# Moving the load, sums and splits of the first w1 chunk, and giving one product of the first feed-forward step its own PSUM bank

## The chip, the cores and the metric

The kernel runs on one core of a Trainium2 chip. TensorE (PE) multiplies into eight PSUM banks of 128 partitions by 512 float32, with its weight loads shown apart as PEld. VectorE (DVE), ScalarE (ACT) and GpSimd (POOL) do the elementwise work. SyncE (SP) issues nearly all DMAs, in program order on one queue. The metric is device time in microseconds (us) of one execution; lower is better. Each engine runs its own instructions in order, so an instruction that waits holds up everything behind it on its engine.

## The reference

The input x is 2048 tokens by 576. The output mixes a linear-attention block and an MLP with a gate of each token:

```python
x = A_x                                             # (1, 2048, 576)
g = sigmoid((x * gate_w).sum(-1, keepdims=True))
q, k, v = split(x @ wqkv)                           # 32 heads of 18
phi = lambda t: where(t > 0, t + 1, exp(t)) + 1e-6
kv = einsum("bhsd,bhse->bhde", phi(k), v);  z = phi(k).sum over tokens
a  = (einsum(phi(q), kv) / (phi(q) . z + 1e-6)) @ wo
y  = layernorm(x)
h  = gelu(y @ w1 + b1)                              # 576 -> 4608, tanh form
b  = h @ w2 + b2                                    # 4608 -> 576
out = g * a + (1 - g) * b
```

All inputs are float32. The kernel keeps that precision by splitting a factor into a high part and a remainder and adding the products high x high, high x low and low x high.

## The kernel before, in words

**Stages.** Up to about 186 us of the profiled span the kernel takes the tokens in 16 blocks of 128, projects keys and queries, and accumulates the sums of phi(k) with x. The next stage, called the wp stage here, turns these sums into one matrix wp (products with `wv`, then `project_values` with `wot`), and then runs 16 steps, `attend(0)` to `attend(15)`, which end at 279.6 us. The rest is the feed-forward: 36 steps k = 0 to 35, two passes over 18 chunks of 256 columns of w1, each pass for 1024 tokens.

**One attend step.** For step i the program issues, in this order: the five PE transposes of block i + 1 (`transpose_q`) with the ACT copies and the two DVE subtractions that make the tile `qt` out of them; the 28 matmuls of `attend(i)`, `ps<-wp,qt`; on DVE `normalize(i + 3)`, which is a reduction, a small addition and a reciprocal on `den` and one wide instruction on the accumulator; on POOL `weigh(i + 4)`, which fills `qz`; on ACT `attend_out(i)`, with a store `late_acc` on SP; and then whatever stands in the list `extra[i]`. A `qt` tile holds high parts, a tail and low parts; the low parts and the lower half of the tail come from the two DVE subtractions, and the matmuls need the tail from the ninth on.

**The first chunks of w1.** Each feed-forward step forms seven products instead of eight from 2 x 2 blocks (Strassen-Winograd), so each chunk of w1 is stored as seven blocks: four are loaded (two DMAs each, eight in all, `accs<-in_um` and `accs<-in_ue`), and four are sums or differences made on POOL by `sum_w1`, each 128x384, the last of which takes the place of a loaded block. Then ACT copies the high parts and DVE subtracts for the low parts (`split_w1`), into `wa` for four blocks and `wb` for three. The raw chunks 0 and 1 use the same place, `spare`, the free front of the tile `accs`. That place holds `xk`, an input of the `wv` products, before. Chunks 0 and 1 are loaded and summed, and chunk 0 is split and stored, inside the attend steps through the lists `extra`: load of chunk 0 at step 1, its sums at 5, its splits at 7 and 9, load of chunk 1 at 9, its sums at 11.

**y.** The normalised and split tokens of the first pass, `y`, are read back from DRAM by seven DMAs of 1280 KB (`load_y`), issued on SP before the attend steps. The place of `y` holds the projection weights of q and k until then, so most of these loads wait for the last projection.

**The feed-forward's order.** `make_up`, `make_units`, `make_w1` and others list operations with what they need and give. A planner then sets the order on every engine by estimated costs and due times: the up-products in the order of the list, the down-products (`ps<-region,h`) merged among them, ACT, DVE and POOL work by due time. A change in one operation's needs can therefore reorder the work of many later steps. In `make_up` a step takes three of the four banks 0 to 3 in turn, called X, Yb and Z: step 0 has banks 0, 1, 2 and step 1 banks 3, 0, 1.

**Step 0 of the feed-forward.** `UP_ORDER` gives the products 1, 5, 6, 2, 7, 4, 3. Product 1 goes to X, 5 to Z, 6 is added to X, 2 goes to Yb, 7 is added to X, 4 is added to X, 3 is added to Z. ACT copies X out to SBUF after product 1 (key u1), after 6 (u2) and after 7 (u3); DVE adds Yb to the first copy (q1) and Z to the third (q3). Product 4 may touch X only when u3 is done, and product 3 may touch Z only when q3 is done. After product 3 DVE adds Z to the second copy (q2). Each of the four results gets a gelu on ACT for the high part, one for the whole, and a DVE subtraction for the low part (`h<-u,h`).

Of the kernel before, what the change touches and what calls it, by code (L numbers as in the profile page):

```python
# [11 lines left out]
AF = mybir.ActivationFunctionType  # L12
# [66 lines left out]
C_OF = {1: (1, 0), 2: (1, 0), 6: (1, 1), 5: (0, 1), 7: (0, 1), 3: (1, 1), 4: (0, 0)}  # L79
W2_PLACES = [FACTORS[n][1] for n in DOWN_ORDER]  # L80
W2_GROUPS = ((0, 1), (2, 3), (4, 5), (6,))

def raw(ap):
# [27 lines left out]
def tile_gated_mix(ctx: ExitStack, tc: tile.TileContext, x, xm, xe, wm, we, wvm, wve, wo, um, ue, w2, b1, b2, gw, out):  # L113
# [22 lines left out]
    def four_times(ap, half):  # L136

        (ld, r), (st, n) = ap.ap
        return bass.AP(tensor=ap.tensor, offset=ap.offset + half * 32 * ld, ap=[[0, 4], [ld, 32], [st, n]])
# [544 lines left out]
            dve.tensor_tensor(out=kvs[:, n, at_:at_ + hi - lo], in0=kv[j][:, own], in1=mask[:, own], op=OP.mult)  # L684
    w_pairs = cycle((6, 4))

    def project_values(t):

        pw = two_of(w_pairs)
        own = [(n, j) for n, (to, j) in enumerate(PIECES) if to == t]  # L690
        for half in range(2):
            for n, j in own:
                pe.matmul(pw[:, half, :HALF], kvs[:, n], wot[:, j, half_cols(half)], start=(n == own[0][0]),
                          stop=(n == own[-1][0]))
        p = pw[:, :, :HALF]
        act.activation(halves(wp[:, t]), p, AF.Copy)
        dve.tensor_tensor(out=halves(wp[:, 5 + t]), in0=p, in1=halves(raw(wp[:, t])), op=OP.subtract)
# [47 lines left out]

    b2b = pks
    hs, wholes = {}, {}

    def wr(k):
        at_ = fresh[:, :21 * P] if k > 1 else spare[:, :21 * P]  # L750
        return at_.rearrange("p (m s n) -> p m s n", m=7, s=3)

    def load_w1(k):
        r = wr(k)
        main = um[k].rearrange("p (h t f n) -> p h t f n", h=2, t=2, f=CF)
        for f, a in ((0, A11), (1, A21)):
            for h in range(2):
                sp.dma_start(r[:, a + h, 0:2], main[:, h, :, f])
                sp.dma_start(r[:, a + h, 2], four_times(ue[k][:, f * P:(f + 1) * P], h))

    def sum_w1(k, which=range(4)):
        r = wr(k)
        for to, x0, x1, op in [((S1, A21, A22, OP.add), (S2, S1, A11, OP.subtract), (S4, A12, S2, OP.subtract),
                                (S3, A11, A21, OP.subtract))[n] for n in which]:
            pool.tensor_tensor(out=r[:, to], in0=r[:, x0], in1=r[:, x1], op=op)
# [51 lines left out]
    def split_all_w1(k, first):  # L817
        a0, a1 = FIRST_W if first else LAST_W
        for part in range(3):
            split_w1(k, a0, a1 + 1, part)  # L820

    extra = {i: [] for i in range(NT)}
    extra[1] += [lambda: load_w1(0)]
    for i, part in ((1, gates_in), (2, gates_act), (3, gates_out)):
        extra[i] += [lambda part=part: part(len(MOMENTS) - 1)]
    extra[5] += [lambda: sum_w1(0), lambda: act.activation(tiny, ones[:, 0:1], AF.Gelu_apprx_tanh)]
    extra[7] += [lambda: split_all_w1(0, True), lambda: store_w1(0, True)]
    extra[9] += [lambda: split_all_w1(0, False), lambda: load_w1(1), lambda: store_w1(0, False)]
    extra[11] += [lambda: sum_w1(1)]
    extra[13] += [lambda: sp.dma_start(b2b, everywhere(b2, D))]  # L830

    for i in range(NT):
# [45 lines left out]
    def op(engine, f, cols=0, needs=(), gives=(), port=False, take=None, give=(), ns=None, tail=None, more=0, by=None,  # L878
           early=0):
        if ns is None:  # L880
            a, b, c = COST[engine]
            ns = a + b * cols + more
            tail = ns + c
        o = Op(engine, f, ns, tail, needs, gives, port, take, give, by)
        o.early = early
        ops.append(o)
        for key in o.gives:
            assert key not in makers, key
            makers[key] = o
        if take:  # L890
            lines[take[0]].append(o)
        return o
# [26 lines left out]
    def add_to(to, x, y):  # L919
        dve.tensor_tensor(out=to, in0=x, in1=y, op=OP.add)  # L920
# [27 lines left out]
    def make_up(k):  # L948
# [3 lines left out]
        w1_in = lambda n: w1_key(k, FACTORS[n][0])  # L952
        seven = k in SEVEN
        base = lambda n: y_in(n) + w1_in(n)
        for n in UP_ORDER:
            if n == 1:
                up_product(k, 1, X, True, base(1) + free(X))
                if k:
# [27 lines left out]
                up_product(k, 4, X, False, base(4) + [("u3", k)])  # L986
                gelu_op(k, H21, lambda: ps[:, X], [("p", k, 4)], not seven, False)
            if n == 3:
                up_product(k, 3, Z, False, base(3) + [("q3", k)])
                op(DVE, lambda: add_to(us((k, H12)), ps[:, Z], us((k, H12))), SB, needs=[("p", k, 3), ("u2", k)],  # L990
                   gives=[("q2", k)])
                gelu_op(k, H12, lambda: us((k, H12)), [("q2", k)], True, True)
            if seven and n in (4, 3):
# [520 lines left out]
```

## Time and profile before

| | us |
|---|---|
| median of 3 runs | 1127.2 |
| lowest and highest | 1127.04 and 1127.81 |
| time of the profiled execution | 1125.78 |
| its span | 1124.1 |
| PE busy in the span | 1108.0 |
| DVE busy | 888.7 |
| ACT busy | 642.6 |
| POOL busy | 385.9 |

The page lists busy time by engine, then groups of instructions. In a timeline a row gives the start, the busy time, the engine and the operation with its count, and in brackets the idle time before it on that engine with the engine and tile that ended it. SPq rows are the DMA issues on SP's queue. Nearly all instructions are recorded through one helper, so they carry line 109; they are told apart by their tiles. `ps` is PSUM, `accs` the tile whose front is `spare`, `region` the split w2, `fresh` the raw chunks of w1 and w2 from the feed-forward on.

### The profile page before, as it was taken

Reading aid. Unit: us, or ns where it says so; the run is one execution under the profiler, and the core shown is the slowest. Engines: PE = TensorE matmul, PEld = TensorE weight load, DVE = VectorE, ACT = ScalarE, POOL = GpSimd, SP = SyncE. Lnnn points to the kernel's source line nnn. Section 1 sums busy time; section 2 is a strip of 40 time slices with the busy share of each in tenths; the row PEclk is TensorE's granted clock in tenths of the full one; section 3 lists DMA queues with packets and bytes.
Section 4 is the critical chain, followed back from the end, with each engine's and each line's share of the span. In section 5 each row is a group of like instructions: output and inputs, shape, how many; then the busy total and the mean of one; then the engine's idle time right before and its main releaser. Section 6 shows DMA issues by size and latency. Waiting matters only on the chain.

```text
span 1124.1 us, 18584 instructions
## 1 busy us (share of the span) xinstructions
PE 1108.0 (99%) x6766; PEld 1003.5 (89%) x6766; DVE 888.7 (79%) x1369; ACT 642.6 (57%) x1153; POOL 385.9 (34%) x325
## 2 busy tenths in 40 slices
PE   9999999999999999999999999999999999999998
PEld 8999889999889888898988888888888888888888
DVE  4567685896787889979979997877887778778888
ACT  6667565453556665666756666345554555455542
POOL 2111112342334252634515453315433443344430
PEclk9999999999999999999999999999999999999999
DMA  6269853554636546473564549764445444444432
GB/s 177 64 88 286 168 171 141 225 204 160 210 122 213 187 162 213 150 267 126 186 221 154 197 166 373 280 234 129 120 123 147 127 115 127 138 127 124 120 109 85
DMA packets 109086, 189.42 MB, mean 169 GB/s; under 512 B 8892, under 2 KB 69068, under 8 KB 104898
## 3 DMA queue, kind: packets, MB, share of 16 engines
q1 hardware_dynamic: 108114, 187.49, 52.7%
q8 instruction: 53, 0.87, 0.3%
q10 hardware_dynamic: 720, 0.74, 0.2%
q14 instruction: 39, 0.32, 0.1%
q0 software_dynamic: 160, 0.01, 0.1%
HBM read 121.40 MB, written 66.80 MB: 167 GB/s over the span
## 4 chain that ended last, share of the span: by engine, by line
PE 72%; DVE 14%; ACT 4%; DMA 4%; issue 3%; POOL 2%; SPq 1%; ACTq 0%; DVEq 0%; POOLq 0%
PE ps L109 72%; DVE accs L109 3%; DVE h L109 3%; DMA fresh<-in_w 2%; DVE region L109 2%; SPq L109 1%; DVE wa L109 1%; POOL u L109 1%; DVE wb L109 1%; DVE den L109 1%; ACT h L109 1%; ACT u L109 1%; POOL fresh L109 1%; DVE u L109 1%; DMA w1d<-wb 0%
## 5 line engine op out<-in xcount | busy, mean ns | idle before, releaser
L109 PEld LDWEIGHTS ps<-region,h 128*128 128x128 f32 x3144 | 453.7, 188 | 45.9 <-DVE accs L109 10.0
L109 PE MATMUL ps<-region,h 128*128 128x288 f32 x3144 | 480.9, 296 | 4.0 <-DVE accs L109 2.0
L109 DVE TENSOR_TENSOR accs<-ps,accs 128x576 f32<-128x576 f32 x336 | 250.3, 752 | 89.8 <-PE ps L109 87.0
L109 POOL TENSOR_TENSOR fresh<-fresh 128x288 f32<-128x288 f32 (+1 forms) x164 | 173.8, 1066 | 406.2 <-DMA fresh<-in_w 332.0
L109 PE MATMUL ps<-y,wa 128*128 128x512 f32 x1008 | 269.7, 393 | 1.4 <-ACT ps L109 1.1
L109 PE MATMUL ps<-y,wb 128*128 128x512 f32 x756 | 204.3, 396 | 1.2 <-ACT u L109 1.0
L109 PEld LDWEIGHTS ps<-y,wa 128*128 128x128 f32 x1008 | 176.3, 188 | 27.2 <-DVE wa L109 1.7
L109 DVE TENSOR_TENSOR h<-u,h 128x512 fp32r<-128x512 f32 x222 | 177.1, 811 | 7.2 <-ACT u L109 4.3
L109 POOL TENSOR_TENSOR u<-u 128x512 f32<-128x512 f32 x104 | 152.3, 1465 | 88.1 <-DVE h L109 46.8
L109 PEld LDWEIGHTS ps<-y,wb 128*128 128x128 f32 x756 | 132.5, 188 | 24.7 <-ACT u L109 1.6
L109 PE MATMUL ps<-y 128*128 128x288 f32 (+1 forms) x896 | 126.9, 297 | 3.6 <-DVE acc L109 2.2
L109 ACT ACTIVATE u<-ps 128x512 f32<-128x512 f32 x73 | 43.7, 598 | 151.4 <-PE ps L109 151.4
L109 PEld LDWEIGHTS ps<-y 128*128 128x128 f32 x896 | 122.3, 188 | 7.0 <-DVE acc L109 3.4
L109 DVE TENSOR_TENSOR region<-fresh,region 128x576 fp32r<-128x576 f32 x120 | 107.8, 898 | 2.4 <-ACT region L109 1.9
L109 ACT ACTIVATE region<-fresh 128x576 fp32r<-128x576 f32 x120 | 73.9, 628 | 33.9 <-PE ps L109 33.9
L109 ACT ACTIVATE h<-ps,b1s 128x512 fp32r<-128x512 f32 x45 | 30.9, 687 | 81.9 <-PE ps L109 81.8
L109 ACT ACTIVATE h<-u,b1s 128x512 fp32r<-128x512 f32 x73 | 52.6, 721 | 32.7 <-DVE u L109 32.7
L109 ACT ACTIVATE h<-u 128x512 fp32r<-128x512 f32 x104 | 60.2, 622 | 12.4 <-POOL u L109 12.2
L109 PE MATMUL ps<-wp,qt 128*128 128x288 f32 x448 | 63.6, 298 | 1.2 <-DVE qt L109 1.2
L109 DVE TENSOR_TENSOR u<-ps,u 128x512 f32<-128x512 f32 x73 | 50.2, 688 | 15.7 <-ACT u L109 12.1
L109 DVE TENSOR_TENSOR wa<-fresh,wa 128x512 fp32r<-128x512 f32 x64 | 50.6, 791 | 14.8 <-ACT wa L109 13.9
L109 PEld LDWEIGHTS ps<-wp,qt 128*128 128x128 f32 x448 | 60.0, 188 | 1.7 <-DVE qt L109 1.7
(122 smaller groups left out, 994.9 us busy)
## 6 DMA issues: line engine op xcount, KB each, us to landing
w1d<-wa SPq DMA_DIRECT2D x17, 1280.0 KB
wa<-w1d SPq DMA_DIRECT2D x68, 320.0 KB
fresh<-in_w SPq DMA_DIRECT2D x70, 288.0 KB
y<-yd SPq DMA_DIRECT2D x14, 1280.0 KB
w1d<-wb SPq DMA_DIRECT2D x17, 960.0 KB
wb<-w1d SPq DMA_DIRECT2D x51, 320.0 KB
yd<-ystage SPq DMA_DIRECT2D x28, 320.0 KB
fresh<-in_um SPq DMA_DIRECT2D x64, 128.0 KB
```

Of the source, the lines that this page charges most:

```text
L109: return lambda *args, **kwargs: self.tc.keep_in_program_order(op(*args, **kwargs))
```

## The change

Four things change.

1. `load_w1(0)`, the eight DMAs of the first raw chunk, is issued right after the masked copies of the `wv` products, ahead of `project_values` and ahead of the seven loads of `y`. Before, it came in `extra[1]`, behind the loads of `y` and two stores.
2. The four sums of chunk 0 stand in `extra[0]` to `extra[3]`, one in each, instead of all four in `extra[5]`.
3. The splits of chunk 0 move from the steps 7 and 9 to 10 and 12; with the second goes the load of chunk 1 (9 to 12), and its sums move from 11 to 14.
4. In feed-forward step 0, product 3 comes before product 4 and opens bank 3 instead of being added to Z. It waits for no copy. DVE adds bank 3 to the second copy (new key q4) and then Z (q2), one DVE addition more. Step 1, whose X is bank 3, waits for q4 before its first product.

```diff
+W1_AT = (10, 12, 14)
+FIRST_ORDER = (1, 5, 6, 2, 7, 3, 4)
...
     w_pairs = cycle((6, 4))
+    def wr(k): ...
+    def load_w1(k): ...
+    load_w1(0)
+
     def project_values(t):
...
-    extra[1] += [lambda: load_w1(0)]
     for i, part in ((1, gates_in), (2, gates_act), (3, gates_out)):
         extra[i] += [lambda part=part: part(len(MOMENTS) - 1)]
-    extra[5] += [lambda: sum_w1(0), lambda: act.activation(tiny, ones[:, 0:1], AF.Gelu_apprx_tanh)]
-    extra[7] += [lambda: split_all_w1(0, True), lambda: store_w1(0, True)]
-    extra[9] += [lambda: split_all_w1(0, False), lambda: load_w1(1), lambda: store_w1(0, False)]
-    extra[11] += [lambda: sum_w1(1)]
+    for n in range(4):
+        extra[n] += [lambda n=n: sum_w1(0, (n,))]
+    extra[5] += [lambda: act.activation(tiny, ones[:, 0:1], AF.Gelu_apprx_tanh)]
+    extra[W1_AT[0]] += [lambda: split_all_w1(0, True), lambda: store_w1(0, True)]
+    extra[W1_AT[1]] += [lambda: split_all_w1(0, False), lambda: load_w1(1), lambda: store_w1(0, False)]
+    extra[W1_AT[2]] += [lambda: sum_w1(1)]
...
-        for n in UP_ORDER:
+        for n in UP_ORDER if k else FIRST_ORDER:
...
-                up_product(k, 3, Z, False, base(3) + [("q3", k)])
-                op(DVE, lambda: add_to(us((k, H12)), ps[:, Z], us((k, H12))), SB, needs=[("p", k, 3), ("u2", k)],
+                up_product(k, 3, Z if k else 3, not k, base(3) + ([("q3", k)] if k else bank_users[3]))
+                if not k:
+                    op(DVE, lambda: add_to(us((k, H12)), ps[:, 3], us((k, H12))), SB, needs=[("p", k, 3), ("u2", k)],
+                       gives=[("q4", k)])
+                    bank_users[3] = [("q4", k)]
+                op(DVE, lambda: add_to(us((k, H12)), ps[:, Z], us((k, H12))), SB, needs=[("p", k, 3), ("u2", k)] if k else [("p", k, 5), ("q4", k)],
                    gives=[("q2", k)])
```

Three places in the order of the built programs follow. On POOL in the attend steps (`qz` is `weigh`, `accs<-accs` a sum of a w1 chunk) the order before is

```order
L109 TENSOR_TENSOR qz<-accs,pks 128x576 x8
L109 TENSOR_TENSOR qz<-acc_93,pks 128x576
L109 TENSOR_TENSOR qz<-acc_94,pks 128x576
L109 TENSOR_TENSOR accs<-accs 128x384 x4
L109 TENSOR_TENSOR qz<-acc_95,pks 128x576
```

and after

```order
L110 TENSOR_TENSOR qz<-accs,pks 128x576 x5
L110 TENSOR_TENSOR accs<-accs 128x384
L110 TENSOR_TENSOR qz<-accs,pks 128x576
L110 TENSOR_TENSOR accs<-accs 128x384
L110 TENSOR_TENSOR qz<-accs,pks 128x576
L110 TENSOR_TENSOR accs<-accs 128x384
L110 TENSOR_TENSOR qz<-accs,pks 128x576
L110 TENSOR_TENSOR accs<-accs 128x384
L110 TENSOR_TENSOR qz<-acc_93,pks 128x576
```

The block of four sums is gone from between the tenth and eleventh `weigh`; each sum now stands between two of them, earlier.

On DVE around the first split of chunk 0 (`den` and `acc` are `normalize`, `qt` the subtractions that the next attend step needs) the order before is

```order
L109 SCALAR_TENSOR_TENSOR acc_95<-acc_95,den 128x576
L109 TENSOR_TENSOR wa<-accs,wa 128x4x256
L109 TENSOR_TENSOR wa<-accs,wa 64x4x128
L109 TENSOR_TENSOR qt<-ps,qt 128x512
L109 TENSOR_TENSOR qt<-ps,qt 64x128
```

and after

```order
L110 SCALAR_TENSOR_TENSOR acc_98<-acc_98,den 128x576
L110 TENSOR_TENSOR wa<-accs,wa 128x4x256
L110 TENSOR_TENSOR wa<-accs,wa 64x4x128
L110 TENSOR_TENSOR qt<-ps,qt 128x512
L110 TENSOR_TENSOR qt<-ps,qt 64x128
```

The two instructions are the same; they now stand behind the normalisation of block 13 instead of block 10. The split into `wb` moves in the same way, from behind block 12 (`acc_97`) to behind block 15 (`acc_100`).

On DVE in feed-forward step 0 (`wa` is the split of chunk 1, `u<-ps,u` the additions q3, q4 and q2, `region` the split of w2, `h` the low parts of the gelus) the order before is

```order
L109 TENSOR_TENSOR u<-ps,u 128x512
L109 TENSOR_TENSOR wa<-accs,wa 64x2x128
L109 TENSOR_TENSOR region<-fresh,region 128x2x288
L109 TENSOR_TENSOR u<-ps,u 128x512
L109 TENSOR_TENSOR h<-u,h 128x512 x3
L109 TENSOR_TENSOR region<-fresh,region 128x2x288
L109 TENSOR_TENSOR h<-u,h 128x512
```

and after

```order
L110 TENSOR_TENSOR u<-ps,u 128x512 x2
L110 TENSOR_TENSOR wa<-accs,wa 64x2x128
L110 TENSOR_TENSOR u<-ps,u 128x512
L110 TENSOR_TENSOR region<-fresh,region 128x2x288
L110 TENSOR_TENSOR h<-u,h 128x512 x2
L110 TENSOR_TENSOR region<-fresh,region 128x2x288
L110 TENSOR_TENSOR h<-u,h 128x512 x2
```

The added addition stands in front, and the first split of w2 moves behind the last addition. On PE behind step 0's products, the first down-product before is

```order
L109 MATMUL ps<-y,wb 128x512 x21
L109 MATMUL ps<-y,wa 128x512 x11
L109 MATMUL ps<-region,h 128x288 x12
L109 MATMUL ps<-y,wa 128x512 x7
L109 MATMUL ps<-region,h 128x288 x12
```

and after

```order
L110 MATMUL ps<-y,wb 128x512 x21
L110 MATMUL ps<-y,wa 128x512 x14
L110 MATMUL ps<-region,h 128x288 x12
L110 MATMUL ps<-y,wa 128x512 x4
L110 MATMUL ps<-region,h 128x288 x12
```

Three more matmuls of step 1 stand ahead of the first down-product. From step 2 on the planner's order on ACT, DVE and POOL differs in many places, by one or two positions each; on PE it differs in a few.

More of the change, by code (lines that the diff above doesn't have):

```diff
@@ L685, in tile_gated_mix, with wr, load_w1 @@
     w_pairs = cycle((6, 4))
+    def wr(k):
+        at_ = fresh[:, :21 * P] if k > 1 else spare[:, :21 * P]
+        return at_.rearrange("p (m s n) -> p m s n", m=7, s=3)
+    def load_w1(k):
+        r = wr(k)
+        main = um[k].rearrange("p (h t f n) -> p h t f n", h=2, t=2, f=CF)
+        for f, a in ((0, A11), (1, A21)):
+            for h in range(2):
+                sp.dma_start(r[:, a + h, 0:2], main[:, h, :, f])
+                sp.dma_start(r[:, a + h, 2], four_times(ue[k][:, f * P:(f + 1) * P], h))
+    load_w1(0)
     def project_values(t):
@@ L747, in tile_gated_mix @@
     hs, wholes = {}, {}
[L749 to L759, printed above, removed]
     def sum_w1(k, which=range(4)):
```

## The prediction

> **What bounds the kernel now.** I read the page's busy times first, then busy time by stretch, then PE's waits, then the timelines around the few gaps.
>
> ```profile
> PE 1108.0 (99%) x6766; PEld 1003.5 (89%) x6766; DVE 888.7 (79%) x1369; ACT 642.6 (57%) x1153; POOL 385.9 (34%) x325
> ```
>
> PE is busy for 1108.0 of 1124.1 us. The change removes no matmul, so it can only win idle time of PE, 16.1 us in all. Busy time by stretch (stretch, its length, then busy us of PE, PEld, DVE, ACT, POOL, clock, DMA share, GB/s) shows where that idle time lies:
>
> ```profile
> 188.00:206.00 18.00, 17.85 (x113) 15.32 (x111) 9.79 (x26) 5.03 (x11) 6.70 (x5) 1.00 0.00 1
> 206.00:236.00 30.00, 29.90 (x232) 29.90 (x232) 26.28 (x55) 14.36 (x35) 7.50 (x6) 1.00 0.85 324
> 236.00:279.00 43.00, 41.75 (x319) 41.06 (x318) 34.04 (x54) 19.36 (x41) 17.77 (x14) 1.00 0.44 159
> 310.00:725.20 415.20, 409.80 (x2419) 364.00 (x2417) 358.94 (x511) 260.67 (x429) 173.11 (x136) 1.00 0.58 202
> ```
>
> In the attend steps PE idles 0.10 + 1.25 us. In the long stretch from 310 to 725.2 us it idles 5.4 us, with DVE busy for 358.94/415.2 = 86%. The gaps in the part that the change touches are these rows of PE's timeline (with the row ahead of each gap):
>
> ```profile
> 248.80 1.30 PE L109 MATMUL ps<-wp,qt 128*128 128x288 f32 x8
> 250.95 1.33 PE L109 MATMUL ps<-wp,qt 128*128 128x288 f32 x8 [0.85 <-DVE qt L109]
> 258.64 1.30 PE L109 MATMUL ps<-wp,qt 128*128 128x288 f32 x8
> 260.34 1.86 PE L109 MATMUL ps<-wp,qt 128*128 128x288 f32 x12 [0.39 <-DVE qt L109]
> 285.97 1.75 PE L109 MATMUL ps<-y,wb 128*128 128x512 f32 x7
> 288.71 3.49 PE L109 MATMUL ps<-y,wb 128*128 128x512 f32 x14 [1.00 <-ACT u L109]
> 294.54 1.64 PE L109 MATMUL ps<-region,h 128*128 128x288 f32 x11
> ```
>
> In attend steps 9 and 11 the ninth matmul waits for `qt`, 0.85 and 0.39 us. In feed-forward step 0 product 4 waits 1.00 us for the copy u3.
>
> **Why the attend steps wait.** DVE's timeline in those steps, and POOL's:
>
> ```profile
> 227.67 0.19 DVE L109 TENSOR_TENSOR den<-den,den 128x32 f32<-128x32 f32 x1
> 240.35 1.01 DVE L109 TENSOR_TENSOR den<-den,den 128x32 f32<-128x32 f32 x1
> 247.91 1.93 DVE L109 TENSOR_TENSOR wa<-accs,wa 128x1024 fp32r<-128x1024 f32 x2
> 249.88 1.02 DVE L109 TENSOR_TENSOR qt<-ps,qt 128x512 fp32r<-128x512 f32 x2
> 253.84 1.02 DVE L109 TENSOR_TENSOR qt<-ps,qt 128x512 fp32r<-128x512 f32 x2
> 257.70 1.53 DVE L109 TENSOR_TENSOR wb<-accs,wb 128x768 fp32r<-128x768 f32 x2
> 259.27 1.02 DVE L109 TENSOR_TENSOR qt<-ps,qt 128x512 fp32r<-128x512 f32 x2
> ```
> ```profile
> 204.90 1.42 POOL L109 TENSOR_TENSOR qz<-accs,pks 128x576 f32<-128x576 f32 x1 [3.02 <-DVE den L109]
> 236.75 4.57 POOL L109 TENSOR_TENSOR accs<-accs 128x384 f32<-128x384 f32 x4 [7.59 <-DMA accs<-in_ue]
> 264.53 4.57 POOL L109 TENSOR_TENSOR accs<-accs 128x384 f32<-128x384 f32 x4 [7.36 <-DMA accs<-in_ue]
> ```
>
> Both waits have a split (1.93 and 1.53 us) directly ahead of the late `qt`. POOL, moreover, stood still 7.59 us for the raw chunk, with `weigh` queued behind; when the sums ran, the small `den` addition took 1.01 us instead of 0.19.
>
> **The change, part by part.** The sum is made on the profiled execution: span 1124.1, time 1125.78; the median of the runs, 1127.2, lies 1.42 above it, and the difference found is put on that median.
>
> Load of chunk 0 ahead of `y`. Eight issues are moved; SP's queue and PE's place beside it:
>
> ```profile
> 180.59 31.40 SPq L109 DMA_DIRECT2D y<-yd  x7
> 232.91 0.55 SPq L109 DMA_DIRECT2D accs<-in_ue  x1
> ```
> ```profile
> 190.64 5.66 PE L109 MATMUL ps<-accs,wv 128*126 128x126 f32 x50
> 227.42 3.95 PE L109 MATMUL ps<-wp,qt 128*128 128x288 f32 x28
> 231.67 3.96 PE L109 MATMUL ps<-wp,qt 128*128 128x288 f32 x28
> ```
>
> The load must wait for the `wv` products to leave `spare`, at 190.64 + 5.66 = 196.3. DMA moved next to nothing from 188 to 206 (share 0.00), so eight issues of about 0.55 us end near 200.7. The last load before was issued at 232.91 and released POOL at 236.75, 3.8 us later, with the `y` traffic in the way; that bounds the landing at about 204.5. The first sum stands behind a `weigh` that ends at 204.90 + 1.42 = 206.3, so POOL does not wait: cost 0. Of the seven `y` loads the first slips from 181 to about 201; the others wait for projections anyway. They have until 279 us: cost 0, with tens of us as cover. The stores `late_acc` and the moments come earlier on SP; nobody waits for them here.
>
> Sums in steps 0 to 3. Four POOL instructions of 4.57/4 = 1.14 us each. POOL is busy 7.50 of 30 us there, so POOL itself has room. On DVE each can hold up an instruction; at most 1.01 - 0.19 = 0.82 us each by the `den` row, at least 0 when they fall beside `qt` or the reduction. I take 0 on the path: a sum follows directly on a `weigh`, when DVE comes to the `qt` of the next block (1.02 us, the same with sums running or not). The Trainium skill, "SBUF — State Buffer", "Who interferes with whom", says that a DVE instruction with two SBUF inputs contends with a GpSimd instruction that reads SBUF; the 0.19 and 1.01 agree, and `qt` with its PSUM input keeps 1.02.
>
> Splits at 10 and 12. ACT's part:
>
> ```profile
> 244.34 0.74 ACT L109 ACTIVATE accs<-ps,g 128x576 f32<-128x576 f32 x1 [0.62 <-PE ps L109]
> 244.98 1.48 ACT L109 ACTIVATE wa<-accs 128x1536 fp32r<-128x1536 f32 x1
> 285.07 1.57 ACT L109 ACTIVATE wa<-accs 128x768 fp32r<-128x768 f32 x2
> ```
>
> At step 7 ACT ended the high part at 246.46, but DVE came to the low part only at 247.91, 1.45 us late, because it was behind. If DVE is on time, the split of step 10 runs like this, counted from the first matmul of the step that needs the `qt` behind it (248.80 in the old place): ACT done at -2.34, DVE split done at -0.4, `qt` done at +0.7, needed after eight matmuls at +1.30. Margin 0.6 us. Is DVE on time? Without a split its step is 253.84 - 249.88 = 3.96 us, PE's is 231.67 - 227.42 = 4.25, so it gains 0.3 us per step, and from step 12 on it has no normalisation at all. I take both waits as gone: -0.85 - 0.39 = -1.24. Bounds: 0 if the waits only move, -1.24 if all goes. The second split is 0.4 us shorter and has 1.0 us of margin.
>
> Chunk 1, three steps later. Its sums slip by about 3 x 4.25 = 12.8 us, from 264.53 to at most 277.3, done by 281.9; ACT first wants them at 285.07. Cost 0, margin 3 us; if it is gone, step 1's split is late by what is missing.
>
> Product 3 in bank 3. Product 7 ends at 285.97 + 1.75 = 287.72. Product 3 no longer waits and covers u3; both products end 0.99 us earlier. ACT shows why product 4 waited:
>
> ```profile
> 287.46 0.72 ACT L109 ACTIVATE h<-u,b1s 128x512 fp32r<-128x512 f32 x1 [0.81 <-DVE u L109]
> 288.08 0.58 ACT L109 ACTIVATE u<-ps 128x512 f32<-128x512 f32 x1
> ```
>
> The copy stood behind a gelu; it ends at 288.66, and product 4 now comes at 289.47. The added DVE addition is 0.69 us of work like its neighbours; product 1 of step 1 waits for it, but it can run from 289.5 to 290.2 and that product comes at 291.2: cost 0, at most 0.7. Late next is the first down-product. Three more matmuls of step 1 (3.49/14 = 0.25 us each) come ahead of it, so it could start at 294.54 - 0.99 + 0.75 = 294.30. It wants two low parts from DVE, the second by its sixth matmul, about 0.7 us later:
>
> ```profile
> 292.85 3.64 DVE L109 TENSOR_TENSOR h<-u,h 128x512 fp32r<-128x512 f32 x3
> ```
> ```profile
> 290.98 4.97 POOL L109 TENSOR_TENSOR fresh<-fresh 128x384 f32<-128x384 f32 x4 [21.88 <-DMA fresh<-in_ue]
> ```
>
> The low parts take 1.21 us each while POOL's sums run, so the second ends at 292.85 + 2.43 = 295.28. If POOL's sums, released by a DMA, keep that pace, the sixth matmul waits 295.28 - 295.00 = 0.28 us. If the split of w2, now ahead of the low parts, costs a turn of 1.2 us as well, the whole 0.99 is lost. I take 0.3, by the first case: -0.7. Bounds -0.99 and 0.
>
> The planner's new order. From step 2 on hundreds of rows change place on DVE and ACT without any work added. What PE waits for from 310 to 730 us (engine and tile waited for, us, times, longest):
>
> ```profile
> PE ps L109 <- ACT ps L109: 2.5, 4, 1.1
> PE ps L109 <- DVE accs L109: 2.0, 5, 0.7
> PE ps L109 <- DVE wa L109: 0.4, 1, 0.4
> PE ps L109 <- DVE wb L109: 0.2, 1, 0.2
> ```
>
> Eleven waits, 5.1 us, 0.46 on average. Nothing in the rows says whether the new order has more or fewer. I take 0, with 1.6 us to either side (three or four waits more or fewer); bounds -5.1, and above an equal +5.1 as an estimate.
>
> Sum: -1.24 - 0.7 + 0 = -1.94 us. 1127.2 - 1.9 = 1125.3; in a profiled execution a span of about 1122.2.
>
> **The rivals.**
>
> Sums against DVE. DVE is tight at step 5, behind the gate work:
>
> ```profile
> 225.83 1.02 DVE L109 TENSOR_TENSOR qt<-ps,qt 128x512 fp32r<-128x512 f32 x2 [1.01 <-ACT qt L109]
> 231.24 1.02 DVE L109 TENSOR_TENSOR qt<-ps,qt 128x512 fp32r<-128x512 f32 x2
> ```
>
> That `qt` ends at 232.26 and is needed at 231.67 + 1.30 = 232.97: reserve 0.71, and 1.01 of idle time before. If all four sums hold DVE for 0.82, PE waits 3.28 - 1.72 = 1.56 us, and the time is 1126.9. It takes sums that meet two-input instructions each time; the order speaks against it. It is the outcome to which the port rule named above would lead if every sum hit.
>
> Split too late at 10. If DVE is as late as before (1.45 us against a margin of 0.6), step 12 waits 0.85 us, as step 9 did: 1126.2. For it: at step 5 DVE comes only 0.71 us ahead of need; against it: 0.3 us gained in each step after.
>
> The planner's draw is bad, slower. At 86% busy DVE comes late to evictions (`accs`) or copies, and waits in steps 2 to 17 about double, +5.1: 1125.3 + 5.1 = 1130.4. It decides once they grow by 1.94 + 2.25 = 4.2 us, from 5.1 to 9.3. For it: the evictions stand in pairs more often in the new DVE order. Against: PE's order hardly changes, and it stays the fuller engine.
>
> The planner's draw is good: half of the 5.1 us go, 1122.8.
>
> **How the numbers follow.** 0.2% of 1127.2 is 2.25 us, about what a measurement tells from no change; faster is below 1124.95, slower above 1129.45. Chances: the forecast 0.52 (1123.7 to 1126.9 with the 1.6 us of the planner's draw; somewhat under half of it beyond the bound), sums against DVE 0.08, split too late 0.09, good draw 0.15, bad draw 0.16. Faster 0.25 + 0.15 = 0.40; slower 0.16; within 0.44. The range, 1122.2 to 1130.0, runs from a little beyond the good draw to nearly all of the bad one, with about 0.07 left out below and 0.13 above.
>
> **What would show it right or wrong.** In the profile after: no idle row before `ps<-wp,qt` matmuls in steps 9 to 15; POOL's sums as single rows of 1.1 us before 225 us, without a wait for `accs<-in_ue`; `den` additions of 0.2 us throughout; no wait for ACT `u` in step 0, but perhaps one of about 0.3 us before or in the first `ps<-region,h` rows; PE idle between 310 and 725 us near 5.4. Wrong it would be if `qt` waits return at step 5 or 12, if the first down-product starts a microsecond late, or if the waits for `accs`, `ps` and `wa` in the long stretch come to 9 us or to 2.

## The result, and the profile after

The kernel before took 1127.81 us (median of five, 1127.04 to 1128.59), the changed kernel 1122.95 us (median of five, 1122.56 to 1124.44). The ratio is 0.9963, with a 95% interval of 0.9951 to 0.9975: about 4.2 us won, between 2.8 and 5.5. The forecast was 1125.3.

The profiled execution of the changed kernel took 1124.44 us, with a span of 1122.7. It is the slowest of the five, while that of before (1125.78) was faster than all others of its kernel. So the two traces differ by only 1.4 us in span, and what follows compares stages, not totals. The page's busy times:

```profile
PE 1106.7 (99%) x6766; PEld 1004.9 (90%) x6766; DVE 894.3 (80%) x1370; ACT 643.7 (57%) x1153; POOL 396.7 (35%) x325
```

PE runs the same 6766 matmuls. Busy time by stretch (columns as before; the attend steps now end at 278.1, so that the third row ends at 277.5):

```profile
188.00:206.00 18.00, 17.84 (x113) 15.37 (x111) 9.75 (x25) 5.06 (x11) 6.65 (x5) 1.00 0.37 117
206.00:236.00 30.00, 29.88 (x228) 29.39 (x228) 27.32 (x53) 13.88 (x34) 14.45 (x11) 1.00 0.79 313
236.00:277.50 41.50, 41.50 (x322) 41.48 (x323) 33.25 (x56) 19.77 (x42) 9.12 (x7) 1.00 0.40 146
310.00:725.20 415.20, 408.86 (x2408) 363.12 (x2407) 357.07 (x508) 258.83 (x425) 169.30 (x135) 1.00 0.57 200
```

In the attend steps the idle time of 1.25 us is gone. In the long stretch it is not smaller but larger, 6.3 us instead of 5.4. PE's timeline around the two parts that the diff touches:

```profile
257.85 3.95 PE L110 MATMUL ps<-wp,qt 128*128 128x288 f32 x28
262.11 3.95 PE L110 MATMUL ps<-wp,qt 128*128 128x288 f32 x28
278.11 6.54 PE L110 MATMUL ps<-y,wa 128*128 128x512 f32 x28
284.49 4.92 PE L110 MATMUL ps<-y,wb 128*128 128x512 f32 x21
...
294.11 1.20 PE L110 MATMUL ps<-region,h 128*128 128x288 f32 x7 [0.75 <-DVE h L110]
...
296.80 1.58 PE L110 MATMUL ps<-region,h 128*128 128x288 f32 x10 [0.32 <-DVE h L110]
```

No attend step waits for `qt`, and the feed-forward starts at 278.11 instead of 279.6. The wait of 1.00 us for the copy u3 is gone from step 0; the first two down-products wait instead, 0.75 and 0.32 us, for low parts. The rows of DVE, POOL and SP's queue behind it, one fence for each:

```profile
210.82 1.58 DVE L110 SCALAR_TENSOR_TENSOR accs<-accs,den 128x576 f32<-128x576 f32 x1
219.40 0.19 DVE L110 TENSOR_TENSOR den<-den,den 128x32 f32<-128x32 f32 x1
259.80 1.95 DVE L110 TENSOR_TENSOR wa<-accs,wa 128x1024 fp32r<-128x1024 f32 x2 [0.81 <-ACT wa L110]
261.77 1.02 DVE L110 TENSOR_TENSOR qt<-ps,qt 128x512 fp32r<-128x512 f32 x2
289.64 1.56 DVE L110 TENSOR_TENSOR region<-fresh,region 128x576 fp32r<-128x576 f32 x1
291.13 2.92 DVE L110 TENSOR_TENSOR h<-u,h 128x512 fp32r<-128x512 f32 x2
```
```profile
206.32 1.52 POOL L110 TENSOR_TENSOR accs<-accs 128x384 f32<-128x384 f32 x1
220.85 1.53 POOL L110 TENSOR_TENSOR accs<-accs 128x384 f32<-128x384 f32 x1
275.53 4.17 POOL L110 TENSOR_TENSOR accs<-accs 128x384 f32<-128x384 f32 x4 [20.40 <-DMA w1d<-wb]
289.57 5.35 POOL L110 TENSOR_TENSOR fresh<-fresh 128x384 f32<-128x384 f32 x4 [9.86 <-PE ps L110]
```
```profile
193.28 0.37 SPq L110 DMA_DIRECT2D accs<-in_um  x1
198.85 13.08 SPq L110 DMA_DIRECT2D y<-yd  x7
```

And what PE waits for from 310 to 730 us, the view on which the planner's term rested:

```profile
PE ps L110 <- DVE accs L110: 3.8, 9, 0.7
PE ps L110 <- ACT ps L110: 1.5, 2, 0.9
PE ps L110 <- ACT u L110: 0.4, 1, 0.4
PE ps L110 <- DVE wa L110: 0.4, 1, 0.4
```

Thirteen waits, 6.1 us, against eleven and 5.1. From their first matmul to the feed-forward's first the attend steps take 67.7 us instead of 69.2, so they explain 1.5 us of the 4.2. Step 0 has exchanged a wait of 1.00 us for two of 1.07 in sum, and the long stretch wins nothing. The rest had to come from somewhere that none of these views shows.

### The profile page after: what moved, and what is told of

Same layout as the page of the kernel before. It is cut to its first block, busy times and chain, and to the rows that moved or that the text cites. A ratio compares the mean times of both kernels' runs of the same rounds, so it can differ in the third digit from the quotient of the medians.

```text
span 1122.7 us, 18570 instructions
## 1 busy us (share of the span) xinstructions
PE 1106.7 (99%) x6766; PEld 1004.9 (90%) x6766; DVE 894.3 (80%) x1370; ACT 643.7 (57%) x1153; POOL 396.7 (35%) x325
## 4 chain that ended last, share of the span: by engine, by line
PE 68%; DVE 16%; DMA 5%; ACT 4%; issue 3%; SPq 2%; POOL 1%; DVEq 0%; ACTq 0%; POOLq 0%
PE ps L110 68%; DVE accs L110 5%; DVE h L110 4%; DVE region L110 2%; SPq L110 2%; DMA yd<-ystage 2%; DVE wb L110 1%; DVE wa L110 1%; DVE u L110 1%; DMA fresh<-in_w 1%; ACT u L110 1%; ACT h L110 1%; POOL u L110 1%; DMA t<-in_xe 1%; DMA accs<-in_xe 0%
## 5 line engine op out<-in xcount | busy, mean ns | idle before, releaser
L110 POOL TENSOR_TENSOR u<-u 128x512 f32<-128x512 f32 x104 | 164.5, 1581 | 97.1 <-DVE h L110 60.3
L110 DVE TENSOR_TENSOR h<-u,h 128x512 fp32r<-128x512 f32 x222 | 189.2, 866 | 5.5 <-ACT u L110 4.8
L110 PEld LDWEIGHTS ps<-y,wb 128*128 128x128 f32 x756 | 132.7, 188 | 23.4 <-ACT u L110 0.9
L110 DVE TENSOR_TENSOR region<-fresh,region 128x576 fp32r<-128x576 f32 x120 | 98.1, 818 | 2.0 <-ACT region L110 1.6
L110 POOL TENSOR_TENSOR pks<-pks,k 128x576 f32<-128x576 f32 x15 | 22.0, 1464 | 110.9 <-DVE k L110 110.9
```

The source lines that it names most:

```text
L110: return lambda *args, **kwargs: self.tc.keep_in_program_order(op(*args, **kwargs))
```

## The experiments

Each kernel was timed beside the kernel before on the same chip, five rounds, in three groups. The kernel before had a median of 1124.72, 1124.94 and 1124.85 us there, with single executions between 1122.5 and 1127.3. Each group ran on a chip of its own. The gains below are taken from the ratios; their intervals reach about 1.2 us to either side, so a difference between two kernels, above all from different groups, is hardly resolved below about 1.5 us. To hold the order fixed, the planner was run twice in some kernels: once without emitting anything, for the step 0 whose order is wanted, and once following that order on every engine. In the code below `queues` are these orders, and `makers` names an operation by what it gives.

**The parts of the change, one at a time.** The changed kernel once more, without an edit:

> The changed kernel again, on the same chip as the three others, so that all four are compared side by side: B - 2.8 to B - 5.5 by the interval measured before. The profile of it on record was one of its slower executions (1124.44 of 1122.56 to 1124.44), that of the kernel before its fastest (1125.78 of 1125.78 to 1128.59); a second profile shows what differs between two executions of one program: if waits of one place differ by 1 to 2 us, the spread is there.

Measured: 1120.23 us, ratio 0.9962 (0.9949 to 0.9975). The gain is there again, 4.3 us.

The moves alone, with step 0 and therefore the planner's orders as before:

```diff
-        for n in UP_ORDER if k else FIRST_ORDER:
+        for n in UP_ORDER:
...
-                up_product(k, 3, Z if k else 3, not k, base(3) + ([("q3", k)] if k else bank_users[3]))
+                up_product(k, 3, Z, False, base(3) + [("q3", k)])
```

> The three moves of the w1 chunks alone: load of chunk 0 ahead of y, its sums in attend steps 0 to 3, splits at 10 and 12, chunk 1 at 12 and 14. Feed-forward step 0 as before, so that the planner's order is word for word that of the kernel before. With B the time of the kernel before on the same chip: the prediction's first term says B - 1.2 us (both qt waits gone, nothing else moved). If the moves carry the whole gain that was measured, B - 3.5 to B - 5. If the gain lies in the bank or in the new order alone, B. In the profile: no idle row before ps<-wp,qt; the 1.0 us wait of product 4 for ACT u still there.

Measured: 1124.52 us, ratio 1.0000 (0.9989 to 1.0011). The waits for `qt` are gone here too, so the feed-forward begins earlier, and yet nothing arrives at the end. This is a miss against the 1.2 us that were expected, though the interval just reaches a gain of 1.2. One place where this kernel loses time is shown below.

Moves and bank, but with every engine in the old order (the new addition q4 put in ahead of q2, product 3 ahead of 4):

```diff
+    queues = {e: [... every operation in the order of the old plan ...] for e in free}
+    at = queues[DVE].index(makers["q2", 0])
+    queues[DVE].insert(at, makers["q4", 0])
```

> The moves and the fourth bank, but every engine's order from the plan of the kernel before: the plan is made with the old step 0 and then followed, with product 3 ahead of product 4 and the added DVE addition right ahead of q2. So this is the changed kernel without the new order. If the bank by itself wins its 0.7 to 1.0 us: e1_moves - 0.7 to - 1.0. If the wait only moves to the low parts, as the profile of the changed kernel has it (0.75 + 0.32 us before the first down-products): e1_moves within 0.3. If the new order carries the rest of the gain: slower than the changed kernel by 2 to 3 us.

Measured: 1123.29 us, ratio 0.9989 (0.9979 to 0.9999): 1.2 us won. The wait for u3 is gone; of the new ones only 0.40 us for an addition of step 0 and 0.20 for a low part stand in its trace.

The opposite: the moves with the new order on every engine, but the old step 0 (no fourth bank).

```diff
-        for n in UP_ORDER if k else FIRST_ORDER:
+        for n in UP_ORDER:
...
+    queues = {e: [... every operation in the order of the new plan, without q4 ...] for e in free}
```

> The moves and the new order, but product 3 added to Z after q3 as before, with no added DVE addition: the changed kernel without the bank, product 3 still ahead of product 4 in the order. Product 3 now waits for q3, so PE should wait 1.5 to 2 us after product 7 (u3, then q3). If the new order of the later steps carries the rest of the gain, the time is at or a little above that of the changed kernel: B - 2 to B - 4. If it carries nothing: e1_moves or up to 1 us above it.

Measured: 1120.87 us, ratio 0.9967 (0.9956 to 0.9979): 3.7 us won. Contrary to what was expected, product 4 stands ahead of product 3 in this kernel too, and its wait for u3 (0.99 us) is there as in the kernel before. So the order of the other instructions takes the moves from 0.0 to -3.7 us. The bank adds -0.6 to that, within what is not resolved.

The bank with its new order, without the moves (load, sums and splits at their old steps):

```diff
-    load_w1(0)
...
+    extra[1] += [lambda: load_w1(0)]
+    extra[5] += [lambda: sum_w1(0), ...]
```

> The bank and the new order without the moves of the w1 chunks. If the terms add: the changed kernel + 1.2 us, B - 2 to B - 3.5, with the qt waits of 0.85 and 0.39 us in attend steps 9 and 11. If the moves win nothing even with the new order: equal to the changed kernel.

Measured: 1121.34 us, ratio 0.9975 (0.9964 to 0.9986): 2.8 us won, 1.5 less than with the moves. That fits what was worked out for them (1.24), but a difference of this size between two groups is not resolved by the times. In its trace the waits for `qt` are back in attend steps 9 and 11, 1.11 and 0.40 us.

**One place where the moves alone lose time: the turn of the passes.** Around 723 us, in step 19, the kernel before has this on PE, ACT and POOL:

```profile
725.15 1.19 PE L109 MATMUL ps<-y,wa 128*128 128x512 f32 x4 [1.10 <-ACT ps L109]
726.23 1.85 PE L109 MATMUL ps<-region,h 128*128 128x288 f32 x12
```
```profile
722.94 1.67 ACT L109 ACTIVATE h<-u 128x512 fp32r<-128x512 f32 x3 [3.04 <-POOL u L109]
724.52 0.57 ACT L109 ACTIVATE ps<-ps 128x512 f32<-128x512 f32 x1
```
```profile
714.05 4.14 POOL L109 TENSOR_TENSOR fresh<-fresh 128x288 f32<-128x288 f32 x4 [14.17 <-DMA fresh<-in_w]
718.15 6.13 POOL L109 TENSOR_TENSOR u<-u 128x512 f32<-128x512 f32 x4
```

PE needs ACT's copy `ps<-ps`. It stands behind three copies `h<-u`, which wait for POOL's sums of u, which stand behind POOL's sums of w2, which wait for a DMA. With the moves alone the same place reads:

```profile
723.15 1.46 PE L109 MATMUL ps<-y,wa 128*128 128x512 f32 x4 [2.51 <-ACT ps L109]
724.41 3.06 PE L109 MATMUL ps<-region,h 128*128 128x288 f32 x12
```

The wait has grown from 1.10 to 2.51 us, by more than the 1.24 that was expected of the moves. PE comes to the place 3.4 us earlier than in the kernel before and the DMA is issued 3.25 us earlier, but POOL's sums of w2 begin only 1.78 us earlier, at 712.27: in this execution the load took about 1.5 us longer. And the twelve matmuls behind it take 3.06 instead of 1.85 us, because the granted clock falls (the same columns by stretch):

```profile
724.00:727.00 3.00, 3.00 (x13) 2.77 (x12) 2.10 (x4) 0.18 (x1) 0.00 (x0) 0.50 0.25 98
```

An earlier PE alone does not make the wait longer. With the moves, the bank and the old orders PE comes to the place 3.9 us earlier (at 720.1) than in the kernel before, and its wait is the old one:

```profile
721.20 1.20 PE L110 MATMUL ps<-y,wa 128*128 128x512 f32 x4 [1.10 <-ACT ps L110]
```

In the changed kernel ACT has the copy ahead of the three, and no PE row around it has a wait:

```profile
722.37 0.58 ACT L110 ACTIVATE ps<-ps 128x512 f32<-128x512 f32 x1 [0.99 <-PE ps L110]
724.50 1.68 ACT L110 ACTIVATE h<-u 128x512 fp32r<-128x512 f32 x3 [1.55 <-POOL u L110]
```

Three runs test that one copy. The kernel before with nothing but the copy ahead:

```diff
+copy_ = makers["u1", 19]
+queues[ACT].remove(copy_)
+queues[ACT].insert(queues[ACT].index(makers["hi", 18, S2]), copy_)
```

> The kernel before with one ACT instruction moved: in feed-forward step 19 the copy u1 (ps<-ps) stands ahead of the three copies h<-u that wait for POOL's sums, as in the new order, instead of behind them. Nothing else differs on any engine. B is the time of the kernel before on the same chip. Theory of the one copy: the gain of the new order is this wait, 1.1 us in the profile of before and 2.5 us with a half clock behind it in that of the moves alone, so B - 1.0 to B - 3. Theory of the whole order (gains scattered over steps 2 to 17): B within 0.7. Theory of the moves: B.

Measured: 1123.8 us, ratio 0.9992 (0.9983 to 1.0002). About 0.9 us, at the edge of what can be told, and less than the 1.0 to 3.0 that the theory of the one copy asked for. The wait of 1.10 us goes, and 0.48 us appears a little later, at the copy that opens the bank of the next down-product.

The changed kernel with the copy back behind the three:

```diff
+queues[ACT].insert(queues[ACT].index(makers["hi", 18, S3]) + 1, copy_)
```

> The changed kernel with the same instruction moved the other way: u1 of step 19 behind the three copies. Theory of the one copy: the gain falls to that of the kernel with the moves, the bank and the old order, B - 0.5 to B - 2, that is 2 to 3.5 us slower than the changed kernel, with a PE wait for ACT ps of 1 to 2.5 us near 721 us in the profile. Theory of the whole order: within 0.7 us of the changed kernel.

Measured: 1121.5 us, ratio 0.9971 (0.9960 to 0.9982), about 1.0 us worse than the changed kernel, which was timed in another group. The theory of the one copy asked for 2 to 3.5, the rival for less than 0.7; the times decide for neither. The wait is back at its place:

```profile
721.32 1.19 PE L110 MATMUL ps<-y,wa 128*128 128x512 f32 x4 [0.83 <-ACT ps L110]
```

The moves, the old orders, and the copy ahead (the edit of the first of these three):

> The moves with the old step 0 and the old order, and u1 of step 19 ahead. The moves alone gave B + 0.0, although both qt waits were gone. Theory of the one copy: what the moves win is given back at this copy, which waits for a DMA through POOL; with the copy ahead it stays won, so about 1.2 us faster than the copy ahead without the moves, B - 2.2 to B - 4.2. If the moves win nothing for another reason: equal to the copy ahead without them.

Measured: 1122.64 us, ratio 0.9984 (0.9974 to 0.9993): 1.8 us won where the moves alone won nothing and the copy alone 0.9; 2.2 to 4.2 were asked for. Here too the wait has moved on, and in this trace it is no shorter than the 1.10 of the kernel before:

```profile
724.88 1.88 PE L110 MATMUL ps<-region,h 128*128 128x288 f32 x12 [1.63 <-ACT ps L110]
```

The three runs leave room for about 1 us at this copy, and none of them shows it beyond what can be told. To the 3.7 us of the kernel with the moves and the full new order 1.9 are still missing.

**What the waits of PE do not show: the second pass.** PE is said to be busy nearly all of the time from 735 to 1100 us in both kernels. But the count of matmuls that fit into this window differs. Before, and then after:

```profile
735.00:1100.00 365.00, 364.83 (x2137) 325.42 (x2136) 287.94 (x404) 193.22 (x323) 142.77 (x124) 1.00 0.46 131
```
```profile
735.00:1100.00 365.00, 365.00 (x2148) 328.26 (x2147) 293.40 (x407) 195.00 (x323) 155.29 (x124) 1.00 0.47 133
```

Eleven matmuls more, at 365/2137 = 0.171 us each, are an estimated 1.9 us (single records can be missing, so the count is good to a few). The waits of the weight loads in that window are, in the kernel before,

```profile
PEld ps L109 <- DVE accs L109: 4.5, 16, 0.5
```

and in the changed kernel there is no such line. One step of the second pass shows the place: weight loads and DVE of before, then of after.

```profile
864.06 0.56 PEld L109 LDWEIGHTS ps<-y,wa 128*128 128x128 f32 x3
864.86 0.83 PEld L109 LDWEIGHTS ps<-region,h 128*128 128x128 f32 x6 [0.24 <-DVE accs L109]
```
```profile
862.79 0.75 DVE L109 TENSOR_TENSOR region<-fresh,region 128x576 fp32r<-128x576 f32 x1
863.46 0.68 DVE L109 TENSOR_TENSOR h<-u,h 128x512 fp32r<-128x512 f32 x1
864.06 1.41 DVE L109 TENSOR_TENSOR accs<-ps,accs 128x576 f32<-128x576 f32 x2
```
```profile
864.66 0.94 PEld L110 LDWEIGHTS ps<-region,h 128*128 128x128 f32 x6
```
```profile
861.40 2.38 DVE L110 TENSOR_TENSOR h<-u,h 128x512 fp32r<-128x512 f32 x2
863.70 1.44 DVE L110 TENSOR_TENSOR accs<-ps,accs 128x576 f32<-128x576 f32 x2
865.06 0.68 DVE L110 TENSOR_TENSOR h<-u,h 128x512 fp32r<-128x512 f32 x1
```

In the old order the second split of w2 and the third low part of h stand ahead of a pair of evictions (`accs<-ps,accs`); the first weight load of the next down-product, whose bank the eviction frees, waits 0.24 us for it. In the new order the split is done earlier, the third low part stands behind the pair, and the load does not wait. It happens once in every step. Two runs put this to the test, in steps 20 to 34 and on DVE alone. The changed kernel with the old order at this place:

```diff
+for step in range(20, 35):
+    split_, low_ = makers["w2", (step, 5)], makers["h", step, S3]
+    queues[DVE].remove(split_)
+    queues[DVE].remove(low_)
+    at = queues[DVE].index(makers["evict", "unit", step, 2, 0])
+    queues[DVE][at:at] = [split_, low_]
```

> The changed kernel, with one thing of the old DVE order put back in steps 20 to 34 of the second pass: the second split of w2 and the third low part of h stand ahead of the first pair of evictions again, as they do in the kernel before, instead of the split in front and the low part behind. Theory A (the loss of about 0.12 us a step in the second pass comes from that eviction: the weight load of the next down-product waits for it): 15 steps by 0.12 to 0.25 us, so the time is 1.8 to 3.7 us above that of the changed kernel (about 1122 to 1124 where the kernel before has 1124.9), and the waits of weight loads on DVE's accs after 735 us, which the changed kernel does not have, come to 4 us or more. Rival B (the place on ACT of the last w2 copy, or the other splits on DVE, makes the difference): the time stays within 0.6 us of 1120.2.

Measured: 1125.52 us, ratio 1.0013 (1.0003 to 1.0024), slower than the kernel before and 5.7 us slower than the changed one. Theory A, and more than it asked for: the loads wait longer than in the kernel before, because the two low parts ahead of the split come later in the new order, by 0.25 us against the weight loads.

```profile
PEld ps L110 <- DVE accs L110: 7.4, 15, 0.5
```
```profile
735.00:1100.00 365.00, 364.06 (x2123) 322.92 (x2122) 293.17 (x403) 192.13 (x319) 148.91 (x123) 1.00 0.44 129
```

Fifteen waits of 0.49 us, one in each of the 15 steps, and 25 matmuls fewer in the window, 4.3 us. PE's own rows still call 364.06 of 365 us busy.

And the opposite, the moves and the copy ahead with the old orders, with the third low part behind the evictions:

```diff
+for step in range(20, 35):
+    low_ = makers["h", step, S3]
+    queues[DVE].remove(low_)
+    queues[DVE].insert(queues[DVE].index(makers["evict", "unit", step, 6, 0]) + 1, low_)
```

> The opposite edit: the moves with step 0 and every order as in the kernel before, the copy of step 19 ahead (1122.6 in its own run, 2.3 us below the kernel before), and now in steps 20 to 34 the third low part of h behind the first pair of evictions on DVE; nothing else. Theory A: the weight loads' waits on DVE accs (4.5 us after 735 us) go, and the time falls by 1.8 to 2.0 us, to about 3.2 to 4.3 us below the kernel before (1120.6 to 1121.7). Rival B: no change, 2.3 us below it (1122.6).

Measured: 1121.01 us, ratio 0.9970 (0.9959 to 0.9981): 3.4 us won, 1.6 more than without this edit (measured in another group). The waits of the weight loads fall from 4.5 us (the value is the same without the edit) to

```profile
PEld ps L110 <- DVE accs L110: 0.2, 1, 0.2
```

One instruction of each of 15 steps, moved by two places, takes away the waits that the planner's new order had taken away in the second pass.

**Two tries at more.** To the last kernel, the copy that opens the bank of step 18's down-product ahead of the last high part on ACT:

```diff
+fork_ = makers["forked", 18, 0]
+queues[ACT].remove(fork_)
+queues[ACT].insert(queues[ACT].index(makers["hi", 18, S4]), fork_)
```

> The kernel of the run before, and on ACT the copy to PSUM of step 18's down-product ahead of the last high part of h of that step, as in the new order. It should take away the wait of 1.6 us that stood at 724.88 us when only the other copy had been moved. If the pass turn is paced by ACT alone, 1.0 to 1.6 us less than the run before (about 1119.5 to 1120.5); if it is paced by the DMA of w2 behind it, at most 0.5 less, and the wait turns up at another tile.

Measured: 1120.64 us, ratio 0.9971 (0.9961 to 0.9980), the same as without it. In its trace the wait is still 0.86 us, where the run before has 0.75. ACT shows why:

```profile
719.75 1.67 ACT L110 ACTIVATE h<-u 128x512 fp32r<-128x512 f32 x3 [2.10 <-POOL u L110]
721.32 0.63 ACT L110 ACTIVATE ps<-ps 128x576 f32<-128x576 f32 x1
```

The copy is ahead of one high part, but still behind the three that wait for POOL, and the matmul starts at 722.01, as it ends. A kernel with this copy ahead of all three was not tried.

The changed kernel, with the first two low parts of step 0 ahead of the split of w2:

```diff
+split_ = makers["w2", (0, 0)]
+queues[DVE].remove(split_)
+queues[DVE].insert(queues[DVE].index(makers["h", 0, (1, 0)]) + 1, split_)
```

> The changed kernel, with the first two low parts of h of step 0 ahead of the first split of w2 on DVE. If the first down-product of step 0 waits for the low part alone (0.25 to 0.75 us, and 0.3 behind it), these waits shrink and the time falls by 0.3 to 1.0 us, to about 1119.5. If it wants the split of w2 as much, the wait moves from h to region and the time stays within 0.3 us of 1120.2, or rises by up to 0.7.

Measured: 1120.41 us, ratio 0.9967 (0.9955 to 0.9980), the same as the changed kernel. The wait moves to the split:

```profile
292.39 1.72 PE L110 MATMUL ps<-region,h 128*128 128x288 f32 x11 [1.16 <-DVE region L110]
```

The first down-product wants the low part and the split, and DVE has both to do. No kernel tried here is faster than the changed one beyond what can be told.

**All traces side by side.** Every kernel left one trace, and the changed one two. The table gives the length of four stretches in us: the attend steps, from the first matmul `ps<-wp,qt` to the first `ps<-y,wa`; and parts of the feed-forward, where each step is counted from its first up-product (a step has 49 up-product matmuls). Step 20 is left out; it takes 22.6 to 22.7 us in all of them.

| kernel | attend steps | steps 0 to 18 | step 19 | step 21 to the end |
|---|---|---|---|---|
| before | 69.2 | 438.7 | 24.1 | 359.0 |
| copy ahead | 69.2 | 437.0 | 23.6 | 359.2 |
| moves | 67.7 | 438.1 | 26.9 | 359.1 |
| moves, bank, old orders | 67.7 | 437.8 | 24.1 | 358.9 |
| moves, copy ahead | 67.7 | 439.8 | 24.6 | 359.1 |
| the same, low part behind the evictions | 67.7 | 439.1 | 23.7 | 356.9 |
| the same, second copy ahead | 67.7 | 436.8 | 24.3 | 356.9 |
| moves, new orders | 67.7 | 440.4 | 23.4 | 356.9 |
| bank, new orders | 69.5 | 437.3 | 23.0 | 357.1 |
| changed | 67.7 | 441.6 | 23.3 | 357.1 |
| changed, second trace | 67.7 | 440.0 | 23.3 | 356.9 |
| changed, copy behind | 67.7 | 437.9 | 23.7 | 357.1 |
| changed, low part ahead | 67.7 | 436.7 | 23.3 | 362.0 |
| changed, low parts of step 0 first | 67.7 | 439.4 | 23.0 | 356.9 |

Two columns hardly scatter. The attend steps are 1.5 us shorter in every kernel that has the moves. From step 21 on, 2.1 us are won wherever the third low part stands behind the evictions, whether the planner put it there or the edit, and where it was put back ahead in the new order this stretch is 2.9 us longer than in the kernel before. These two differences are 3.6 of the 4.2 us. Together they give the measured gain of every kernel to within 0.9 us, except for the moves alone (1.5 worked out in this way, 0.0 measured), whose trace loses 2.8 us in step 19. Step 19 itself, with the copy in it, is 0.7 to 1.1 us shorter under the new orders, and 0.4 of the changed kernel's 0.8 goes when the copy is put back behind; under the old orders the copy ahead gives no steady gain (23.6 to 24.6 us with it, 24.1 in two of three traces without). Steps 0 to 18 scatter by 5 us, with no sign of the order; this scatter hides the smaller terms in the times, and why it is there stays open.

## Why the prediction was right or wrong

The time lay in the range and on the forecast's side, but the likeliest case gave 1.9 us of the 4.2, and the interval (2.8 to 5.5) leaves it out. That the time came out at the good draw (1122.8) is luck, as the term of the planner's order shows. Step by step:

- **Load ahead of y: right.** It was issued from 193.28 on, 3 us earlier than worked out from the `wv` products. The first sum ran at 206.32, directly behind its `weigh`, without a DMA wait, as worked out. The `y` loads followed at 198.85, and no matmul of the feed-forward's start waits for them.
- **Sums in steps 0 to 3: right on the path.** They took 1.01 to 1.54 us each rather than 1.14, and the wide DVE normalisation beside the first took 1.58 us, where the trace before has 0.76; `den` stayed at 0.19, and PE waited for neither.
- **Splits at 10 and 12: right, with its margin.** DVE had the split ready for `qt` at 261.77 + 1.02 = 262.79, and the ninth matmul came at 262.11 + 1.30 = 263.41: 0.6 us, as forecast. DVE was so early that it waited 0.81 us for ACT. The -1.24 is there: the attend steps are 1.5 us shorter in every trace with the moves.
- **Chunk 1: right.** Its sums ran from 275.53 to 279.70, before ACT wanted them.
- **The bank: sign uncertain in the trace, within its bounds in time.** The 1.00 us wait went, as forecast. The 0.28 us that I let the first down-product give back was 0.75 + 0.32 in the trace after. The alternative that was named and not taken came about: POOL's sums began at 289.57 instead of 290.98, the split of w2 took 1.56 us beside them, and each low part 1.46 instead of 1.21. By medians the bank is worth 0.6 us in the new order and 1.2 in the old; against the 0.7 forecast neither can be told apart.
- **The planner's new order: the step that failed.** "I take 0, with 1.6 us to either side" should have been -3.7 by the times (moves with old order against moves with new order, 1124.52 to 1120.87). The time of the good draw came out, but not by its mechanism: the waits between 310 and 730 us did not halve, they rose from 5.1 to 6.1 us. What the new order is shown to win is 2.1 us in the second pass, where it puts one eviction of each step ahead of a low part. The term could not see this place. "Waits in steps 2 to 17" left out the second pass, and the premise that the change "can only win idle time of PE" excluded it: PE idled 0.17 us from 735 to 1100 us, and what was lost there lay in waits of its weight loads. Up to about 1 us more may lie at the copy at the turn of the passes. It stood as the longest row of `PE ps <- ACT ps` (1.1) among those I quoted, and I did not follow it to its chain. What is left of the 3.7 is not traced to a place.
- **Terms that add up: not refuted.** The -1.24 was put on the end time as if nothing behind it could take it back. The attend steps did get 1.5 us shorter each time, and the kernels with the moves show it in their times as far as these can tell, all but the one with the moves alone (0.0). Its trace loses more than that in step 19, with a late load and a half clock behind it. Five of its twelve executions had a mean granted clock of 0.998, and two of 27 of the kernel before had one as low or lower; why stays open.

## What to carry to other kernels

An engine that is 99% busy in the records can still lose time: count its instructions in a window of fixed length in both traces, and read the waits of its weight loads beside its own. Before a gain early in a program is put on the end time, look for the next place that is paced by a DMA or another engine, and ask whether the instruction that the bound engine needs there stands behind the one that waits; there a late load can take back what was won before. Where an edit makes a planner sort anew, the new order is part of the change, and holding each engine to the old order in one kernel and to the new in another separates the two. Where whole times scatter by more than the effect, compare the lengths of stages between the same matmuls in all traces: some of them repeat to 0.2 us.

## What the hardware showed unexpectedly

A gap of 2.51 us on PE at 723 us was followed by about 3 us at a granted clock of 0.50, and cost some 1.2 us more on the twelve matmuls behind it alone (3.06 against 1.85); a gap of 1.10 us at the same place, in the kernel before, left the clock at 1.00, and so did the 1.63 us of the kernel with moves and copy. Of the twelve executions with the moves alone, the five with a mean granted clock of 0.998 over the span had a median of 1125.84 us, the seven at 1.000 one of 1124.06. The Trainium skill, "TensorE: Matmul & The Clock Gate", "What's actually happening", gives an idle window of about 3.4 us as what brings the half clock. Here a gap of 2.51 us was enough in the one execution that has a trace, and the measurement decides; where the other four lost their clock is not shown.

Short waits of weight loads cost PE less than they show, but not nothing, and PE's own rows do not show them. A step of the second pass takes 22.59 to 22.60 us without such a wait, 22.67 to 22.71 with one of about 0.25 us, and 22.91 to 22.94 with one of 0.48 or 0.49 (traces of the kernel before, the changed one, the two with the low part moved, and the one with the moves and the copy). So about 0.15 us of each wait cost nothing, and the rest came on top of the step in full. The 7.4 us of waits in the kernel with the low part put back come to 5.0 us of time in this way.
